# An accumulating DMA from GpSimd in place of a VectorE subtraction, in a spectral layer with a rational feed-forward block

## The chip, the cores and the metric

One core of one Trainium2 chip. The metric is device time in microseconds (us) of one execution of the kernel; the kernel before takes 1489.2 us, the median of three runs (1488.56 to 1489.77).

## The reference

The input is `x` of 4 x 3008 x 256. A real FFT runs along the sequence, each frequency's 256 channels go through a complex 256 x 256 mix with a soft threshold of 0.01, and the inverse FFT brings the sequence back. Then each of the 12032 tokens goes through a feed-forward block with a rational activation:

```
y = irfft(soft(rfft(x) @ (w_r + i w_i) + b))          # 4 x 3008 x 256
h = y @ w_in                                          # 12032 x 2048
P = a0 + a1*h + a2*h^2 + a3*h^3
Q = 1 + |b0|*|h| + |b1|*h^2 + 1e-6
out = (P / Q) @ w_out                                 # 12032 x 256
```

## The kernel before

**Blocks and units.** The tokens are cut into 26 blocks of 470 (the last has 282). A block goes through 8 units of 256 hidden channels each, so there are 208 units. A unit's tiles are 128 x 2 x 470, that is 128 x 940 (in the last block 128 x 564). The main loop (line 723) runs over the units in turn; in iteration i it issues the first product of unit i+1, the activation of units i, i-1 and i-2, and the second product of unit i-3. Everything is issued by hand in this order, and each engine works through its own list in order.

**One unit.** `g1_mm` (line 364): 12 matmuls of 470 columns give `h` in PSUM; two such tiles exist. ScalarE (`act_a`, `act_b`): m = |h| (line 394), w = |b1| m + |b0| (397), t = a3 h + a2 (398), then in the next iteration y = (v + C0)^2 (404) and its reciprocal square root (406), which is 1/Q. GpSimd: v = w m (399), so Q = v + C0. VectorE (`dve_a`): t = t h (411), t = (t + a1) h (413), so P = t + a0.

**Two ways to finish a unit** (`dve_b`). In mode "C" the quotient is split in two parts, both in a 32-bit format that TensorE multiplies in one pass: hi = (t + a0) y (423), p = (v + C0) hi (426), t = (t + a0) - p (428), lo = t y (431): six VectorE operations with the two of `dve_a`. The second product `g2_mm` (464) then has 12 matmuls: the high and low half of `w_out` with hi, the high half with lo. In mode "4" VectorE refines y twice (434, 436) and writes one full-precision tile g (440): five operations, and the second product has 4 matmuls of four passes each, shown in the profile as 8 records.

**Which unit takes which.** All units take "C" as long as FFT work of the later sequences is left. Once it is used up (`alone`), the table `TAIL = "4C444C44"` gives six of the eight units of a block mode "4". For these GpSimd joins halves of `w_out` again (line 801).

**FFT work beside the units.** The first sequence's FFT, mix and inverse stand before the loop. Those of the other three are cut into tasks (`fft_tasks`), which a planner spreads over the units by cost, so that TensorE's work per unit is level. Each block also needs its last inverse step (`i2_task`, lines 330 and 247), issued at units 5 and 6 of the block before. All DMAs are issued from SyncE.

**VectorE's order.** In iteration i: t h and (t + a1) h of unit i (any FFT step between them), line 428 of unit i-2, line 423 of unit i-1, line 431 of unit i-2, line 426 of unit i-1. GpSimd's v of unit i may overwrite its buffer only when line 426 (or 436) of unit i-2 has read it.

Of the kernel before, what the change touches and what calls it, by code (L numbers as in the profile page):

```python
# [25 lines left out]
FU = 2  # L26
UB = NFC // FU
LAM = 0.01
MODES = "CCCCCCCC"
TAIL = "4C444C44"  # L30
WARM = 38
FILL = 8
HC = (0, 0, 3, 3, 3, 3, 3, 3, 3, 3, 3, 3)
HM = (0, 0, 4, 4, 4, 4, 4, 4, 4, 4, 4, 4, 0, 0)
I2Q = (5, 6)
SPLIT = [q for q in range(UB) if MODES[q] != "4"]
WHOLE = [q for q in range(UB) if MODES[q] == "4"]
BACK = [q for q in SPLIT if TAIL[q] == "4"]
C0 = float(np.float32(1.0) + np.float32(1e-6))


# [59 lines left out]
def spectral_moe(ctx, tc, t, out):  # L101
# [17 lines left out]
    wout = const.tile([128, len(WHOLE), FU, D], F32, name="wout") if WHOLE else None  # L119
    win = {}  # L120
    wsp = {}
    back = f2.rearrange("p k f -> p (k f)").rearrange("p (k i f) -> p k i f", i=FU, f=D)
    ca, cna, cb = (small[:, k:m] for k, m in ((264, 268), (268, 272), (272, 274)))

    v32 = lambda ap: ap.bitcast(F32)
    early = [1]
# [218 lines left out]
    def width(u):  # L345
        return len(blocks[u // UB]) * TJ
# [20 lines left out]
    joined = []  # L367
    alone = []

    def mode(u):  # L370
        if u not in modes:
            q = u % UB
            four = TAIL[q] == "4" and (q in WHOLE or q in joined) and u != nb * UB - 1
            modes[u] = MODES[q] if not alone else "4" if four else "C"
        return modes[u]

    modes = {}
    rate = {}

    def load_rates():  # L380
        for k, src in (("b", cb[:1, 1:2]), ("a", ca[:1, 3:4]), ("na", cna[:1, 3:4])):
            rate[k] = nc.scalar.alloc_register(f"rate_{k}")
            nc.scalar.reg_load(rate[k], src.bitcast(I32))

    def fresh(nm, bufs):
        return mp.tile([128, FU, TB], F32, tag=nm, name=nm, bufs=bufs)

    def act_a(u):
        w = width(u)
# [24 lines left out]

    def dve_b(u):
        d = un[u]
        w = width(u)
        y, v, tt = (d[k] for k in ("y", "v", "t"))
        stt = nc.vector.scalar_tensor_tensor
        a0 = d["a"][:, 0:1]  # L420
        if mode(u) == "C":
            hi = fresh("g", 4)[:, :, :w].bitcast(F32R)
            stt(out=hi, in0=tt, scalar=a0, in1=y, op0=ALU.add, op1=ALU.mult)  # L423
            yield
            p = fresh("p", 1)[:, :, :w]
            stt(out=p, in0=v, scalar=C0, in1=v32(hi), op0=ALU.add, op1=ALU.mult)  # L426
            yield
            stt(out=tt, in0=tt, scalar=a0, in1=p, op0=ALU.add, op1=ALU.subtract)  # L428
            yield
            lo = fresh("g", 4)[:, :, :w].bitcast(F32R)  # L430
            nc.vector.tensor_tensor(out=lo, in0=tt, in1=y, op=ALU.mult)  # L431
            d["g"] = (hi, lo)
        else:
            stt(out=v, in0=v, scalar=C0, in1=y, op0=ALU.add, op1=ALU.mult)  # L434
            yield
            stt(out=y, in0=v, scalar=-2.0, in1=y, op0=ALU.add, op1=ALU.mult)  # L436
            yield
            yield
            g = fresh("g", 4)[:, :, :w]
            stt(out=g, in0=tt, scalar=a0, in1=y, op0=ALU.add, op1=ALU.mult)  # L440
            d["g"] = (g,)
# [4 lines left out]
    def g2_mm(u):  # L446
        n, q = divmod(u, UB)
        w = width(u)
        if n not in acc:
            acc[n] = [ps1.tile([128, 512], F32, tag=f"acc{e}", name=f"acc{e}") for e in range(2)]  # L450
            begun[n] = 0
        g = un.pop(u)["g"]
        ops = []
        for i in range(FU):
            if len(g) == 2:
                wh, wl = (wsp[q][:, i, z, :] for z in range(2))
                ops += [(wh, g[0][:, i]), (wh, g[1][:, i]), (wl, g[0][:, i])]
            else:
                w1 = wout[:, WHOLE.index(q), i, :] if q in WHOLE else back[:, BACK.index(q), i, :]
                ops.append((w1, g[0][:, i]))  # L460
# [39 lines left out]
    def from_f64(raw, kind, q):  # L500
# [11 lines left out]
        if kind == "whole":  # L512
            tt(out=wout[:, WHOLE.index(q)].rearrange("p k f -> p (k f)").bitcast(U32), in0=e, in1=r, op=ALU.add)
            yield
            return
# [9 lines left out]
    with tc.manual_schedule():  # L525
# [47 lines left out]
        jobs += [("whole", q, w_out[:, FU * q:FU * q + FU, :]) for q in WHOLE]  # L573
        jobs += [("wsp", q, w_out[:, FU * q:FU * q + FU, :]) for q in SPLIT]
        raws = []
        running = []

        def more_raw(n):
            for kind, q, src in jobs[len(raws):len(raws) + n]:
                if kind == "whole":  # L580
                    raw = raw_pool.tile([128, 2, 256], mybir.dt.int64, tag="raw", name="raw")
                else:
                    raw = const.tile([128, 2, 256], mybir.dt.int64, tag=f"{kind}{q}", name=f"raw_{kind}{q}")
# [59 lines left out]
        for p in range(np_ + 3):  # L643
# [79 lines left out]
        for i in range(-1, nu + 4):  # L723
# [59 lines left out]
            for g in live:  # L783
                drain(g)
            drain(da)
            next(prev, None)
            if i >= nu:
                drain(prev)
            next(db, None)
            drain(prev)  # L790
            next(db, None)
            held -= freed
            if len(cur) < 8 and 1 < nextb < B and (nextb, 0) not in xin:
                load_x(nextb, 0)
                load_x(nextb, 1)
            if i >= 0 and not cur and nextb == B:
                alone.append(1)
            left = [z for j, z in enumerate(BACK) if z not in joined and f2_done.get(B - 1, 0) >= 2 * j + 2]
            if left and not storing(i):
                j = BACK.index(left[0])  # L800
                nc.gpsimd.tensor_tensor(out=back[:, j], in0=v32(wsp[left[0]][:, :, 0]), in1=v32(wsp[left[0]][:, :, 1]), op=ALU.add)
                joined.append(left[0])
# [31 lines left out]
```

## Time and profile before

| | us |
|---|---|
| median of three runs | 1489.2 |
| the profiled execution | 1491.45 |
| its span in the profile | 1489.7 |
| TensorE busy | 1464.5 (98%) |
| VectorE busy | 1386.9 (93%) |
| ScalarE busy | 1214.5 (82%) |
| GpSimd busy | 478.4 (32%) |

In the span there are three stretches after a start of 120 us: the units with FFT work beside them (120.1 to 1119.1 us), the 56 units without it (to 1449.1 us), and the last block with what follows it. TensorE's granted clock is 1.00 of full speed in both long stretches. Busy times of VectorE and ScalarE hold a small overlap: an operation that does not depend on the one before starts some 0.08 us before that one's end.

### The profile page before, as it was taken

To read this page: it belongs to the slowest core of one execution; us is meant where nothing else is said; L and a number is where in the kernel's file an instruction comes from. 1 tells how busy PE (TensorE), PEld (TensorE's weight loads), DVE (VectorE), ACT (ScalarE), POOL (GpSimd) and SP (SyncE) were. 2 spreads that over 40 slices of the span, in tenths; PEclk is the share of its full clock that TensorE was granted. 3 is DMA by queue.
4 is the path that set the end of the run, shared out by engine and by line. 5 is a ranking of instruction groups with operands and counts; after the bars stand their busy time and mean duration, and the time that the engine had idled before them with its cause. 6 is when DMAs were issued, how large, how long until landed. Compare 5 with 4: busy or idle time off the path is not lost.

```text
span 1489.7 us, 19526 instructions
## 1 busy us (share of the span) xinstructions
PE 1464.5 (98%) x7323; PEld 1221.7 (82%) x7325; DVE 1386.9 (93%) x1347; ACT 1214.5 (82%) x1555; POOL 478.4 (32%) x230
## 2 busy tenths in 40 slices
PE   8999999999999999999999999999999999999998
PEld 4886999999888999999888998988987777777776
DVE  2667899999999999999999999999999999999998
ACT  2767888888888888888888888888888888888885
POOL 0102222332323233332323334333333333433332
PEclk9999999999999999999999999999999999999999
DMA  8934111111232111111232101011010000000000
GB/s 261 374 114 143 45 42 56 33 51 41 70 104 78 33 37 55 32 52 41 69 100 77 34 28 55 28 35 41 26 44 16 24 14 27 27 14 27 8 14 22
DMA packets 53458, 89.00 MB, mean 60 GB/s; under 512 B 4939, under 2 KB 37459, under 8 KB 53363
## 3 DMA queue, kind: packets, MB, share of 16 engines
q1 hardware_dynamic: 53363, 87.75, 19.0%
q8 instruction: 58, 0.95, 0.3%
q14 instruction: 37, 0.30, 0.1%
HBM read 50.25 MB, written 37.49 MB: 59 GB/s over the span
## 4 chain that ended last, share of the span: by engine, by line
PE 74%; DVE 11%; issue 7%; ACT 3%; DMA 0%; POOL 0%; SPq 0%; ACTq 0%; DVEq 0%; POOLq 0%
PE acc L464 30%; PE h L364 28%; PE pft L268 6%; PE pi L330 3%; DVE t L411 3%; DVE t L428 2%; DVE p L426 2%; PE pft L171 2%; PE pft L286 2%; PE pft L225 2%; DVE t L413 1%; PE pi L247 1%; DVE y L436 1%; DVE v L434 1%; PE pft L247 0%
## 5 line engine op out<-in xcount | busy, mean ns | idle before, releaser
L399 POOL TENSOR_TENSOR v<-w,m 128x940 f32<-128x940 f32 (+1 forms) x208 | 455.8, 2191 | 913.3 <-DVE p L426 514.5
L364 PE MATMUL h<-xsh,win 128*128 128x470 f32 (+1 forms) x1664 | 449.9, 392 | 2.5 <-DVE t L413 2.2
L464 PE MATMUL acc<-g,wsp 128*128 128x470 f32 (+1 forms) x1908 | 433.2, 375 | 3.4 <-DVE g L431 3.1
L464 PEld LDWEIGHTS acc<-g,wsp 128*128 128x128 f32 x1908 | 357.5, 189 | 53.5 <-DVE g L431 5.6
L364 PEld LDWEIGHTS h<-xsh,win 128*128 128x128 f32 x1664 | 304.2, 190 | 63.2 <-issue 23.6
L411 DVE TENSOR_TENSOR t<-t,h 128x940 f32<-128x940 f32 (+1 forms) x208 | 231.1, 1111 | 29.0 <-ACT t L398 28.8
L404 ACT ACTIVATE y<-v 128x940 f32<-128x940 f32 (+1 forms) x207 | 201.9, 975 | 66.8 <-POOL v L399 66.1
L413 DVE SCALAR_TENSOR_TENSOR t<-t,small,h 128x940 f32<-128x940 f32 (+1 forms) x208 | 244.8, 1177 | 6.1
L394 ACT ACTIVATE m<-h 128x940 f32<-128x940 f32 (+1 forms) x208 | 195.4, 939 | 60.5 <-PE h L364 55.4
L364 PE MATMUL h<-xsl,win 128*128 128x470 f32 (+1 forms) x832 | 242.0, 372 | 0.0
L397 ACT ACTIVATE w<-m,small 128x940 f32<-128x940 f32 (+1 forms) x208 | 220.1, 1058 | 0.0
L398 ACT ACTIVATE t<-h,small 128x940 f32<-128x940 f32 (+1 forms) x208 | 212.3, 1021 | 0.0
L406 ACT ACTIVATE y<-y 128x940 f32<-128x940 f32 (+1 forms) x207 | 202.5, 978 | 0.0
L423 DVE SCALAR_TENSOR_TENSOR g<-t,small,y 128x940 fp32r<-128x940 f32 (+1 forms) x158 | 192.6, 1219 | 0.0
L428 DVE SCALAR_TENSOR_TENSOR t<-t,small,p 128x940 f32<-128x940 f32 (+1 forms) x159 | 188.3, 1184 | 0.0
L431 DVE TENSOR_TENSOR g<-t,y 128x940 fp32r<-128x940 f32 (+1 forms) x158 | 178.0, 1127 | 10.9 <-PE acc L464 10.7
L426 DVE SCALAR_TENSOR_TENSOR p<-v,g 128x940 f32<-128x940 f32 (+1 forms) x159 | 178.5, 1122 | 0.2
L364 PEld LDWEIGHTS h<-xsl,win 128*128 128x128 f32 x832 | 155.2, 188 | 20.7 <-DVE xsl L341 0.2
L464 PE MATMUL acc<-g,f 128*128 128x470 f32 (+1 forms) x392 | 156.8, 542 | 1.5 <-DVE g L440 1.4
L464 PEld LDWEIGHTS acc<-g,f 128*128 128x128 f32 x392 | 73.5, 189 | 60.0 <-issue 52.7
L268 PE MATMUL pft<-wrh,x 128*128 128x256 f32 x288 | 76.5, 288 | 0.8 <-ACT pft L155 0.8
L268 PE MATMUL pft<-wih,x 128*128 128x256 f32 x288 | 75.0, 283 | 0.0
(94 smaller groups left out, 1450.1 us busy)
## 6 DMA issues: line engine op xcount, KB each, us to landing
xin<-in_x SPq DMA_DIRECT2D x32, 384.0 KB, 4.2
s<-zt SPq DMA_DIRECT2D x48, 256.0 KB, 2.2
out_t<-ob SPq DMA_DIRECT2D x50, 235.0 KB, 2.2
ct<-s SPq DMA_DIRECT2D x21, 480.0 KB, 4.6
s<-a SPq DMA_DIRECT2D x48, 192.0 KB, 2.8
bt<-s SPq DMA_DIRECT2D x36, 256.0 KB, 2.9
raw_win<-in_w_in SPq DMA_DIRECT2D x8, 512.0 KB, 10.6
raw_wsp<-in_w_out SPq DMA_DIRECT2D x8, 512.0 KB, 8.7
```

The costliest lines, as they stand in the source:

```text
L268: nc.tensor.matmul(out=pt[:, k, :], lhsT=l, rhs=r, start=False, stop=n == len(ops) - 1, skip_group_check=True)
L364: nc.tensor.matmul(out=h[:, i, :w], lhsT=l, rhs=r, start=k == 0, stop=k == len(halves) // FU - 1)
L397: nc.scalar.activation(out=d["w"], in_=d["m"], func=ACTF.Identity, scale=rate["b"], bias=cb[:, 0:1])
L398: nc.scalar.activation(out=d["t"], in_=h, func=ACTF.Identity, scale=rate["a" if mode(u) == "C" else "na"], bias=a[:, 2:3])
L399: nc.gpsimd.tensor_tensor(out=d["v"], in0=d["w"], in1=d["m"], op=ALU.mult)
L404: nc.scalar.activation(out=d["y"], in_=d["v"], func=ACTF.Square, bias=C0)
L406: nc.scalar.activation(out=d["y"], in_=d["y"], func=ACTF.Abs_reciprocal_sqrt)
L411: nc.vector.tensor_tensor(out=tt, in0=tt, in1=h, op=ALU.mult)
L413: nc.vector.scalar_tensor_tensor(out=tt, in0=tt, scalar=d["a"][:, 1:2], in1=h, op0=ALU.add, op1=ALU.mult)
L426: stt(out=p, in0=v, scalar=C0, in1=v32(hi), op0=ALU.add, op1=ALU.mult)
L428: stt(out=tt, in0=tt, scalar=a0, in1=p, op0=ALU.add, op1=ALU.subtract)
L464: nc.tensor.matmul(out=acc[n][e][:, :w], lhsT=l[:, e * 128:(e + 1) * 128], rhs=r, start=begun[n] == 1 and k == 0, stop=begun[n] == UB and ...
```

## The change

Line 428 goes. In its place `p` is written into `v` with the other sign, and GpSimd issues a DMA that adds the 128 x 940 tile `v` to `t` in SBUF. lo then takes (t + a0) y in one step. The signs are turned by loading w as -(|b1| m + |b0|) (`ncb`), so that v = -(Q - C0); y = (v - C0)^2 is unchanged. The tiles `w` and `p` go; `v` gets 4 buffers in place of 2, and the pieces `g` 5 in place of 4. Mode "4", its table and the join on GpSimd go: every unit is split. The very last unit adds on VectorE. In the loop both steps of unit i-1 (hi, p) now come before lo of unit i-2.

```diff
-        for nm, bufs in (("m", 2), ("w", 2), ("t", 4), ("v", 2)):
+        for nm, bufs in (("m", 2), ("v", 4), ("t", 4)):
...
-        nc.scalar.activation(out=d["w"], in_=d["m"], func=ACTF.Identity, scale=rate["b"], bias=cb[:, 0:1])
...
-        nc.gpsimd.tensor_tensor(out=d["v"], in0=d["w"], in1=d["m"], op=ALU.mult)
+        nc.scalar.activation(out=d["v"], in_=d["m"], func=ACTF.Identity, scale=rate["b"], bias=ncb[:, 0:1])
+        nc.scalar.activation(out=d["t"], in_=h, func=ACTF.Identity, scale=rate["a"], bias=ca[:, 2:3])
+        nc.gpsimd.tensor_tensor(out=d["v"], in0=d["v"], in1=d["m"], op=ALU.mult)
...
-        if mode(u) == "C":
...
+        piece = lambda: fresh("g", 5)[:, :, :width(u)].bitcast(F32R)
+        hi = piece()
+        stt(out=hi, in0=tt, scalar=ca[:, 0:1], in1=y, op0=ALU.add, op1=ALU.mult)
+        yield
+        stt(out=v, in0=v, scalar=-C0, in1=v32(hi), op0=ALU.add, op1=ALU.mult)
+        if u == nb * UB - 1:
+            nc.vector.tensor_tensor(out=tt, in0=tt, in1=v, op=ALU.add)
+        else:
+            nc.gpsimd.dma_start(out=tt, in_=v, accum_op=ALU.add)
+        yield
+        lo = piece()
+        stt(out=lo, in0=tt, scalar=ca[:, 0:1], in1=y, op0=ALU.add, op1=ALU.mult)
+        d["g"] = (hi, lo)
...
             drain(da)
-            next(prev, None)
-            if i >= nu:
-                drain(prev)
+            next(db, None)
             next(db, None)
             drain(prev)
-            next(db, None)
+            if i >= nu:
+                drain(db)
```

VectorE before, two neighbouring units of the stretch without FFT work (the numbers are buffers of the tiles; equal numbers are one tile):

```order
L411 TENSOR_TENSOR t_10074<-t_10074,h_10017 128x940
L413 SCALAR_TENSOR_TENSOR t_10074<-t_10074,small_69,h_10017 128x940
L434 SCALAR_TENSOR_TENSOR v_10033<-v_10033,y_10077 128x940
L440 SCALAR_TENSOR_TENSOR g_10090<-t_9989,small_69,y_10035 128x940
L436 SCALAR_TENSOR_TENSOR y_10077<-v_10033,y_10077 128x940
L411 TENSOR_TENSOR t_10111<-t_10111,h_10059 128x940
L413 SCALAR_TENSOR_TENSOR t_10111<-t_10111,small_69,h_10059 128x940
L423 SCALAR_TENSOR_TENSOR g_10126<-t_10074,small_69,y_10114 128x940
L440 SCALAR_TENSOR_TENSOR g_10128<-t_10032,small_69,y_10077 128x940
L426 SCALAR_TENSOR_TENSOR p_10130<-v_10075,g_10126 128x940
```

The same place now:

```order
L392 TENSOR_TENSOR t_10073<-t_10073,h_10012 128x940
L394 SCALAR_TENSOR_TENSOR t_10073<-t_10073,small_69,h_10012 128x940
L402 SCALAR_TENSOR_TENSOR g_10095<-t_10027,small_69,y_10075 128x940
L404 SCALAR_TENSOR_TENSOR v_10026<-v_10026,g_10095 128x940
L411 SCALAR_TENSOR_TENSOR g_10099<-t_9975,small_69,y_10029 128x940
L392 TENSOR_TENSOR t_10116<-t_10116,h_10058 128x940
L394 SCALAR_TENSOR_TENSOR t_10116<-t_10116,small_69,h_10058 128x940
L402 SCALAR_TENSOR_TENSOR g_10138<-t_10073,small_69,y_10118 128x940
L404 SCALAR_TENSOR_TENSOR v_10072<-v_10072,g_10138 128x940
L411 SCALAR_TENSOR_TENSOR g_10142<-t_10027,small_69,y_10075 128x940
```

Line 402 (hi) and line 404, which reads the hi just written, are now neighbours; before, an operation on another unit's tiles stood between lines 423 and 426. Line 411 (lo) reads the t to which the DMA of the iteration before has added.

GpSimd before, in the same stretch:

```order
L399 TENSOR_TENSOR v_10724<-w_10722,m_10721 128x940
L399 TENSOR_TENSOR v_10760<-w_10758,m_10757 128x940
L399 TENSOR_TENSOR v_10796<-w_10794,m_10793 128x940
L399 TENSOR_TENSOR v_10839<-w_10837,m_10836 128x940
L399 TENSOR_TENSOR v_10889<-w_10887,m_10886 128x940
```

and now:

```order
L380 TENSOR_TENSOR v_10297<-v_10297,m_10296 128x940
L408 DMA t_10247<-v_10246 128x940
L380 TENSOR_TENSOR v_10348<-v_10348,m_10347 128x940
L408 DMA t_10298<-v_10297 128x940
L380 TENSOR_TENSOR v_10400<-v_10400,m_10399 128x940
L408 DMA t_10349<-v_10348 128x940
```

Between two multiplications there is now the issue of a DMA, for the unit two before the one multiplied next (in iteration i: v of unit i, then the DMA of unit i-1, then v of unit i+1).

## Rows read from the trace of the kernel before

**Rows 1.** The page, its busy times: us, share, instructions.

```profile
PE 1464.5 (98%) x7323; PEld 1221.7 (82%) x7325; DVE 1386.9 (93%) x1347; ACT 1214.5 (82%) x1555; POOL 478.4 (32%) x230
```

**Rows 2.** By stretch: start:end, length, busy PE, PEld, DVE, ACT, POOL; clock, DMA share, GB/s.

```profile
120.10:1119.10 999.00, 992.52 (x5229) 876.05 (x5230) 965.79 (x894) 851.23 (x1083) 332.03 (x150) 1.00 0.17 52
1119.10:1449.10 330.00, 329.04 (x1324) 237.32 (x1323) 321.64 (x295) 277.23 (x323) 123.83 (x56) 1.00 0.06 19
```

**Rows 3.** VectorE's line 411 by stretch, once per unit: busy (count).

```profile
120.10:1119.10 999.00, 162.29 (x144) 1.00 0.17 52
1119.10:1449.10 330.00, 62.91 (x56) 1.00 0.06 19
```

**Rows 4.** Chain that ended last, 880 to 905 us, by line.

```profile
by line: PE acc L464 41.3%; PE h L364 32.6%; PE pft L268 12.4%; PE pi L330 4.5%; PE pft L225 3.6%; PE pft L286 3.5%; PE pi L247 1.7%; PE pft L247 0.9%
```

**Rows 5.** Waits of TensorE for VectorE, 120 to 1119 us: total, times, longest.

```profile
PE h L364 <- DVE t L413: 1.4, 2, 0.8
...
PE acc L464 <- DVE g L431: 0.2, 1, 0.2
```

**Rows 6.** Chain around one block without FFT work: start us, us, what.

```profile
1208.59 3.16 PE acc L464 x8
...
1214.31 2.56 PE acc L464 x12
1216.87 2.59 PE h L364 x12
...
1239.18 1.13 PE pi L330 x10
...
1242.88 0.21 PE pi L247
```

**Rows 7.** VectorE in order of time in that block: start us, us, what.

```profile
1218.12 1.12 DVE L436 SCALAR_TENSOR_TENSOR y<-v,y 128x940 f32<-128x940 f32 x1
1219.17 1.12 DVE L411 TENSOR_TENSOR t<-t,h 128x940 f32<-128x940 f32 x1
1220.32 1.19 DVE L413 SCALAR_TENSOR_TENSOR t<-t,small,h 128x940 f32<-128x940 f32 x1
...
1222.50 1.19 DVE L440 SCALAR_TENSOR_TENSOR g<-t,small,y 128x940 f32<-128x940 f32 x1
1223.61 1.13 DVE L436 SCALAR_TENSOR_TENSOR y<-v,y 128x940 f32<-128x940 f32 x1
```

**Rows 8.** VectorE at the start of the loop, lines 423 and 426 as neighbours.

```profile
126.94 1.19 DVE L423 SCALAR_TENSOR_TENSOR g<-t,small,y 128x940 fp32r<-128x940 f32 x1
128.24 1.14 DVE L426 SCALAR_TENSOR_TENSOR p<-v,g 128x940 f32<-128x940 f32 x1
```

**Rows 9.** GpSimd in order of time, same block.

```profile
1219.39 2.19 POOL L399 TENSOR_TENSOR v<-w,m 128x940 f32<-128x940 f32 x1 [3.30 <-DVE y L436]
```

**Rows 10.** ScalarE in order of time, same block.

```profile
1221.62 0.99 ACT L404 ACTIVATE y<-v 128x940 f32<-128x940 f32 x1 [0.88 <-POOL v L399]
...
1223.48 1.02 ACT L398 ACTIVATE t<-h,small 128x940 f32<-128x940 f32 x1
```

**Rows 11.** SyncE's issue of one DMA, in order of time.

```profile
568.53 0.46 SPq L314 DMA_DIRECT2D ct<-s  x1
```

**Rows 12.** DMA issues: count, KB each, median us from issue to landing.

```profile
out_t<-ob SPq DMA_DIRECT2D x50, 235.0 KB, 2.2
ct<-s SPq DMA_DIRECT2D x21, 480.0 KB, 4.6
```

**Rows 13.** VectorE in the last block, in order of time.

```profile
1469.21 0.74 DVE L411 TENSOR_TENSOR t<-t,h 128x564 f32<-128x564 f32 x1
...
1472.74 0.73 DVE L411 TENSOR_TENSOR t<-t,h 128x564 f32<-128x564 f32 x1
...
1481.47 0.80 DVE L423 SCALAR_TENSOR_TENSOR g<-t,small,m 128x564 fp32r<-128x564 f32 x1
1482.38 0.75 DVE L426 SCALAR_TENSOR_TENSOR p<-v,g 128x564 f32<-128x564 f32 x1
```

More of the change, by code (lines that the diff above doesn't have):

```diff
@@ L28 @@
 LAM = 0.01
-MODES = "CCCCCCCC"
-TAIL = "4C444C44"
 WARM = 38
@@ L35 @@
 I2Q = (5, 6)
-SPLIT = [q for q in range(UB) if MODES[q] != "4"]
-WHOLE = [q for q in range(UB) if MODES[q] == "4"]
-BACK = [q for q in SPLIT if TAIL[q] == "4"]
 C0 = float(np.float32(1.0) + np.float32(1e-6))
@@ L118, in spectral_moe @@
     wmix = {n: const.tile([128, 2, D], F32R, name=n) for n in ("wrh", "wrl", "wih", "wil")}
-    wout = const.tile([128, len(WHOLE), FU, D], F32, name="wout") if WHOLE else None
     win = {}
     wsp = {}
-    back = f2.rearrange("p k f -> p (k f)").rearrange("p (k i f) -> p k i f", i=FU, f=D)
-    ca, cna, cb = (small[:, k:m] for k, m in ((264, 268), (268, 272), (272, 274)))
+    ca, ncb, cb = (small[:, k:m] for k, m in ((264, 268), (268, 270), (272, 274)))
     v32 = lambda ap: ap.bitcast(F32)
@@ L365, in g1_mm @@
         un[u] = {"h": h}
[L367 to L377, printed above, removed]
     rate = {}
     def load_rates():
-        for k, src in (("b", cb[:1, 1:2]), ("a", ca[:1, 3:4]), ("na", cna[:1, 3:4])):
+        for k, src in (("b", ncb[:1, 1:2]), ("a", ca[:1, 3:4])):
             rate[k] = nc.scalar.alloc_register(f"rate_{k}")
@@ L395, in act_a @@
         yield
-        d["a"] = a = ca if mode(u) == "C" else cna
-        nc.scalar.activation(out=d["w"], in_=d["m"], func=ACTF.Identity, scale=rate["b"], bias=cb[:, 0:1])
-        nc.scalar.activation(out=d["t"], in_=h, func=ACTF.Identity, scale=rate["a" if mode(u) == "C" else "na"], bias=a[:, 2:3])
-        nc.gpsimd.tensor_tensor(out=d["v"], in0=d["w"], in1=d["m"], op=ALU.mult)
+        nc.scalar.activation(out=d["v"], in_=d["m"], func=ACTF.Identity, scale=rate["b"], bias=ncb[:, 0:1])
+        nc.scalar.activation(out=d["t"], in_=h, func=ACTF.Identity, scale=rate["a"], bias=ca[:, 2:3])
+        nc.gpsimd.tensor_tensor(out=d["v"], in0=d["v"], in1=d["m"], op=ALU.mult)
     def act_b(u):
@@ L403, in act_b @@
         d["y"] = fresh("m", 2)[:, :, :width(u)] if u == nb * UB - 1 else fresh("y", 3)[:, :, :width(u)]
-        nc.scalar.activation(out=d["y"], in_=d["v"], func=ACTF.Square, bias=C0)
+        nc.scalar.activation(out=d["y"], in_=d["v"], func=ACTF.Square, bias=-C0)
         yield
@@ L412, in dve_a @@
         yield
-        nc.vector.scalar_tensor_tensor(out=tt, in0=tt, scalar=d["a"][:, 1:2], in1=h, op0=ALU.add, op1=ALU.mult)
+        nc.vector.scalar_tensor_tensor(out=tt, in0=tt, scalar=ca[:, 1:2], in1=h, op0=ALU.add, op1=ALU.mult)
     def dve_b(u):
         d = un[u]
-        w = width(u)
         y, v, tt = (d[k] for k in ("y", "v", "t"))
         stt = nc.vector.scalar_tensor_tensor
-        a0 = d["a"][:, 0:1]
-        if mode(u) == "C":
[L422 to L432, printed above, removed]
-        else:
[L434 to L441, printed above, removed]
+        piece = lambda: fresh("g", 5)[:, :, :width(u)].bitcast(F32R)
[5 more added lines that the diff above has]
+            nc.vector.tensor_tensor(out=tt, in0=tt, in1=v, op=ALU.add)
+        else:
+            nc.gpsimd.dma_start(out=tt, in_=v, accum_op=ALU.add)
[3 more added lines that the diff above has]
+        d["g"] = (hi, lo)
     acc = {}
@@ L454, in g2_mm @@
         for i in range(FU):
[L455 to L460, printed above, removed]
+            wh, wl = (wsp[q][:, i, z, :] for z in range(2))
+            ops += [(wh, g[0][:, i]), (wh, g[1][:, i]), (wl, g[0][:, i])]
         begun[n] += 1
@@ L493, in spectral_moe @@
     pro3 = pro_stack.enter_context(tc.tile_pool(name="pro3", bufs=3))
-    raw_pool = pro_stack.enter_context(tc.tile_pool(name="raw", bufs=len(WHOLE))) if WHOLE else None
     pro2 = pro_stack.enter_context(tc.tile_pool(name="pro2", bufs=2))
@@ L511, in from_f64 @@
         yield
[L512 to L515, printed above, removed]
         tt(out=e, in0=e, in1=r, op=ALU.add)
@@ L572, in spectral_moe @@
         jobs = [("win", q, w_in[:, :, 256 * q:256 * q + 256]) for q in range(UB)]
-        jobs += [("whole", q, w_out[:, FU * q:FU * q + FU, :]) for q in WHOLE]
-        jobs += [("wsp", q, w_out[:, FU * q:FU * q + FU, :]) for q in SPLIT]
+        jobs += [("wsp", q, w_out[:, FU * q:FU * q + FU, :]) for q in range(UB)]
         raws = []
@@ L579, in more_raw @@
             for kind, q, src in jobs[len(raws):len(raws) + n]:
[L580 to L583, printed above, removed]
+                raw = const.tile([128, 2, 256], mybir.dt.int64, tag=f"{kind}{q}", name=f"raw_{kind}{q}")
                 nc.sync.dma_start(out=raw, in_=src)
@@ L687, in spectral_moe @@
             if p == 8:
-                nc.vector.tensor_scalar(out=cna, in0=ca, scalar1=-1.0, scalar2=None, op0=ALU.mult)
                 nc.scalar.activation(out=cb, in_=cb, func=ACTF.Abs)
+                nc.vector.tensor_scalar(out=ncb, in0=cb, scalar1=-1.0, scalar2=None, op0=ALU.mult)
         load_rates()
@@ L716, in load @@
         def load(i):
-            z = 0.5 * storing(i) + 2.36 + (0.0 if i < 3 else 3.16 if MODES[(i - 3) % UB] == "4" else 2.36)
+            z = 0.5 * storing(i) + 2.36 + (0.0 if i < 3 else 2.36)
             return z + (1.24 if i % UB in I2Q else 0.0)
@@ L795, in spectral_moe @@
                 load_x(nextb, 1)
[L796 to L802, printed above, removed]
             if 0 <= i < nu and q == 1 and n + 1 < nb:
```

## The prediction

> **What bounds the kernel now.** I read the page's busy times first, then the busy times by stretch, then the chain of waits inside each long stretch, and only then single instructions in order of time. The page shows two engines near full: TensorE at 98% and VectorE at 93% [rows 1]. An average does not say which of them sets the pace, so the next view is by stretch.
>
> In the stretch with FFT work TensorE is busy 992.5 of 999.0 us, VectorE 965.8 [rows 2]. The chain there, followed back, holds TensorE lines alone [rows 4], and TensorE waited for VectorE for 1.4 + 0.2 = 1.6 us in all of it [rows 5]. The reader is to see that VectorE, though almost full, delays nobody there: a faster VectorE can give back those 1.6 us and little more.
>
> The stretch without FFT work has 56 units in 330.0 us [rows 2, 3], 5.89 us each. The chain around one block shows TensorE without a gap: six second products of mode "4" at 3.16 us, two of mode "C" at 2.56, eight first products at about 2.57, two inverse steps of 1.13 + 0.21 [rows 6]: 18.96 + 5.12 + 20.56 + 2.68 = 47.3 us for 8 units, 5.92 each, which is the measured pace. Here too TensorE sets it, but with work that the change takes away.
>
> **The change part by part.**
>
> *TensorE.* In the FFT stretch its list is the same. Without FFT work six of eight second products go from 3.16 to 2.56 us: 8 x 2.56 + 20.56 + 2.68 = 43.7 us per block, 5.47 per unit. If nothing else bound, that would be worth 56 x (5.89 - 5.47) = 24 us.
>
> *VectorE.* A unit now takes five operations everywhere. I take the distance from start to start, since ends overlap the next start. Line 411 to 413, which reads what 411 has just written, is 1.15 us; an operation with the coefficient column to its independent neighbour is 1.11 (440 to 436); one with a constant is 1.05 (436 to 411) [rows 7]. The new neighbours hi and p depend on each other. Lines 423 and 426 stood so once at the loop's start, 1.30 us apart [rows 8], 0.19 more than hi costs now. So a unit takes 1.15 + 1.11 + 1.30 + 1.05 + 1.11 = 5.72 us. In the FFT stretch VectorE's 965.8 us over 144 units are 6.71 per unit; less 1.11 for the subtraction, plus 0.19, plus 0.06 because lo now carries the coefficient column, that is 5.85, against a pace of 999.0 / 144 = 6.94. Cover is ample there, and TensorE stays the wall: gain 1.6 us. Without FFT work 5.72 is above TensorE's 5.47, so VectorE becomes the bound: 56 x 5.72 = 320.3 in place of 330.0, gain 9.7 us.
>
> *The DMA, its latency.* lo of a unit stands one whole iteration behind the p that starts its DMA: between them lie lo of the unit before, two steps of `dve_a`, hi and p, 5.72 us of VectorE. A latency L up to that costs nothing. Beyond it VectorE waits W in each iteration, with L = 5.72 + 2W, because the wait lengthens the iteration it hides in; so a unit costs (L - 5.72) / 2 more. Queued behind the waiting lo are `dve_a` of the next unit (which frees `h` for the first product after) and hi. In the FFT stretch L may reach 5.85 + 2 x (6.94 - 5.85) = 8.0 before TensorE feels it. No accumulating DMA is in this trace. Nearest rows: 235 KB from SBUF land after 2.2 us, 480 KB into SBUF after 4.6 [rows 12]; this one moves 481 KB and reads its destination too. Ends: 2.2 + 0.46 = 2.7 us, and twice 4.6 plus an issue of 2.2, 11.4. I take the row with the same size, 4.6, plus the issue below: L = 5.6, just inside. The Trainium skill ("DMA: Bandwidth & Descriptors", section on the anatomy of one DMA) gives for a DMA from GpSimd about 2.0 us plus the bytes at 436 GB/s, by which 481 KB would take an estimated 3.1 us and the sum would be the same.
>
> *The DMA, its issue on GpSimd.* While GpSimd issues (d), v of the next unit waits behind it. The loop: the last reader of v, line 436, ends at 1219.24 [rows 7], GpSimd starts at 1219.39 and takes 2.19 [rows 9], ScalarE's square starts at 1221.62, its t ends at 1224.50 [rows 10]: 5.26 us. In the new order line 404 releases the DMA, so d comes in; then `dve_a`, hi and p follow, 1.15 + 1.11 + 1.30 + 1.13 = 4.69, and about 0.1 for the start. The whole, 10.05 + d, has two units to run in: a pace of 5.72 allows d up to 1.4 us. In the FFT stretch two units are 13.9 us and d may be near 3. Bounds for d: SyncE's issue, 0.46 [rows 11], and a whole GpSimd multiplication, 2.19 [rows 9]; I take 1.0, the geometric middle. Below nothing it cannot be, since it stands in GpSimd's list.
>
> *The rest.* Of the buffers, v of unit i also waits for the DMA of unit i-4, more than two units earlier, which costs nothing at the L taken. lo comes after hi and p now; the second product that reads it stands two iterations behind, as before. In the last block a unit takes 3.53 us on VectorE, five operations of about 0.71; the pair hi, p is 0.91 apart there [rows 13], so 8 x 0.2 = 1.6 us more, and at the end lo of the last unit but one waits for its DMA with little before it: 0.9, together +2.5. The copies, constants and joins that go (GpSimd's, off the path) count nothing.
>
> *Sum.* -1.6 - 9.7 + 2.5 = -8.8 us. The profiled execution took 1491.45 us (span 1489.7), 2.25 above the median; 1482.65 less 2.25 is 1480.4: I predict 1480 us.
>
> **The rivals.**
>
> *A. GpSimd becomes the bound (slower).* For it: GpSimd is in the loop with 0.4 us to spare at d = 1.0, and ScalarE already waits 0.88 us for v in this block [rows 10]. Against: GpSimd idles 3.30 us before each multiplication [rows 9]. At d = 2.2, the upper bound, a unit takes (10.05 + 2.2) / 2 = 6.12: 56 x 0.23 = 13 us lost without FFT work, with -1.6 and +2.5 about 1503 us. It decides for slower from d = 1.7 (5.88 a unit). GpSimd's multiplication runs its 2.19 us beside lines 411 and 413, which keep their 1.15 us and 1.19 us [rows 7, 9], so the trace shows no stop of a whole operation. The Trainium skill ("SBUF — State Buffer", section "Who interferes with whom") says that a VectorE operation with two SBUF inputs and a GpSimd one that reads SBUF block each other for the whole operation; if issuing were held so, d would be an estimated 1.0 + 1.2, which is this rival.
>
> *B. The transfer is late (slower).* If the second read costs a third of the transfer more, L is 1.0 + 1.3 x 4.6 = 7.0 and a unit takes 6.36: 56 x 0.47 = 26, about 1516 us. It turns the change from L = 6.0. The DMA engines are far from full (share 0.06 without FFT work [rows 2]), which speaks against queueing; the unknown rate of adding speaks for it. At L = 11.4 a unit would take 8.6 in both stretches, (8.6 - 6.94) x 144 + (8.6 - 5.89) x 56 = 390 us more; nothing points there.
>
> *C. TensorE keeps the pace.* If hi and p stand closer than 1.30 (p's wait was seen once), VectorE falls to TensorE's 5.47: 24 us in place of 9.7, about 1466 us.
>
> *D. A draw.* L or d lies just past its limit, a unit takes 5.85 to 5.95, and the gain is eaten: about 1489 us.
>
> **How the numbers follow.** Forecast 0.43 (its own range 1474 to 1486), A 0.15, B 0.17, C 0.13, D 0.12. A measurement tells no change from about 0.2%, 3 us. Faster: forecast and C, 0.56; same: D, 0.12; slower: A and B, 0.32. The range goes from C, 1466, to short of B, 1512; what lies outside is most of B and a tail of C.
>
> **What would show it.** After: TensorE's busy share in the FFT stretch unchanged and that stretch within 3 us of 999.0; units without FFT work 5.7 us apart with VectorE full and TensorE waiting about 0.25 us per unit; lines 402 and 404 1.30 apart; no wait of line 411 for the DMA; GpSimd's issue near 1 us. Wrong would be: waits of line 411 for DMA in most units (B), waits of ScalarE's square for GpSimd that grow by more than 0.4 us per unit (A), units at 5.5 (C), or an FFT stretch that moves by over 5 us either way.

## The result and the profile after

The changed kernel takes 1507.25 us (median of four runs, 1501.95 to 1511.85), against 1489.33 for the kernel before beside it: a ratio of 1.012, interval 1.0085 to 1.0155. It became slower by about 18 us; the forecast was 1480. The profiled execution took 1508.81 us, its span is 1507.0.

The busy times of the page after, beside [rows 1], and four of its groups (line, engine, operation, count | busy us, mean ns | idle before, releaser):

```profile
PE 1450.8 (96%) x7521; PEld 1259.8 (84%) x7521; DVE 1272.3 (84%) x1189; ACT 1214.2 (81%) x1555; POOL 656.5 (44%) x431
...
L380 POOL TENSOR_TENSOR v<-v,m 128x940 f32<-128x940 f32 (+1 forms) x208 | 501.3, 2410 | 73.5 <-ACT v L378 50.4
L408 POOL DMA_DIRECT2D t<-v x207 | 184.6, 892 | 684.7 <-DVE v L404 684.7
...
L411 DVE SCALAR_TENSOR_TENSOR g<-t,small,y 128x940 fp32r<-128x940 f32 (+1 forms) x207 | 264.5, 1278 | 17.0 <-DMA t<-v 15.6
L402 DVE SCALAR_TENSOR_TENSOR g<-t,small,y 128x940 fp32r<-128x940 f32 (+1 forms) x207 | 253.0, 1222 | 1.6 <-ACT y L387 1.6
...
t<-v POOLq DMA_DIRECT2D x200, 470.0 KB, 4.4
...
out_t<-ob SPq DMA_DIRECT2D x50, 235.0 KB, 3.9
ct<-s SPq DMA_DIRECT2D x21, 480.0 KB, 6.3
```

VectorE lost 115 us of work; besides TensorE's weight loads (PEld) only GpSimd has more to do than before. The two numbers that the prediction did not have came out near its choice: the issue takes 0.89 us (1.0 was taken), the transfer lands 4.4 us after it (4.8 after line 404's end; 5.6 was taken, 5.72 was the limit). The transfers beside it became slower, `out_t` from 2.2 to 3.9 us and `ct` from 4.6 to 6.3 [rows 12]; none of the waits below is for those. What stands out is the mean of line 411: 1278 ns, where the other operations of its kind take 1.19 us.

The same three stretches, cut where VectorE starts units 0, 144 and 200 (columns as in [rows 2]):

```profile
116.40:1120.20 1003.80, 994.17 (x5224) 879.62 (x5225) 842.11 (x753) 850.37 (x1082) 447.57 (x288) 0.99 0.55 120
1120.20:1457.20 337.00, 316.75 (x1493) 269.28 (x1491) 324.86 (x282) 277.00 (x322) 176.39 (x114) 0.98 0.49 99
1457.20:1507.00 49.80, 34.09 (x205) 30.57 (x203) 41.15 (x47) 24.57 (x40) 21.09 (x17) 0.92 0.43 76
```

Before they were 999.0, 330.0 and 40.6 us. So the stretch with FFT work lost 4.8 us, the 56 units without it 7.0, the last block 9.2; the start gave 3.7 back. Together that is the 17.3 us between the spans.

**One unit in some twenty.** VectorE after, in order of time (start us, us, what, [idle before, releaser]):

```profile
1298.64 1.13 DVE L392 TENSOR_TENSOR t<-t,h 128x940 f32<-128x940 f32 x1
1299.81 1.19 DVE L394 SCALAR_TENSOR_TENSOR t<-t,small,h 128x940 f32<-128x940 f32 x1
1300.92 1.26 DVE L402 SCALAR_TENSOR_TENSOR g<-t,small,y 128x940 fp32r<-128x940 f32 x1
1302.29 1.14 DVE L404 SCALAR_TENSOR_TENSOR v<-v,g 128x940 f32<-128x940 f32 x1
1304.04 3.92 DVE L411 SCALAR_TENSOR_TENSOR g<-t,small,y 128x940 fp32r<-128x940 f32 x1 [0.61 <-DMA t<-v]
1307.88 1.12 DVE L392 TENSOR_TENSOR t<-t,h 128x940 f32<-128x940 f32 x1
```

and GpSimd in the same place:

```profile
1298.64 2.53 POOL L380 TENSOR_TENSOR v<-v,m 128x940 f32<-128x940 f32 x1
1303.84 0.89 POOL L408 DMA_DIRECT2D t<-v  x1 [2.67 <-DVE v L404]
1304.45 2.50 POOL L380 TENSOR_TENSOR v<-v,m 128x940 f32<-128x940 f32 x1
```

lo (line 411) waited 0.61 us for its transfer, and then took 3.92 us in place of 1.19. It ends at 1307.96; GpSimd's multiplication (line 380) ends at 1306.95, 1.01 us earlier. Read hi (line 402) against the multiplication before it: that ends at 1301.17, hi at 1302.18, 1.01 us later again, and hi took 1.26 us. Both look as if VectorE's work on them began only when GpSimd was done (1.01 us is close to the 1.19 that such an operation takes alone). The unit cost 9.24 us from one line 392 to the next; its neighbours take 5.81. Nine of the 207 lo's are this long (2.3 to 3.95 us), and all nine end 1.0 us after a multiplication's end.

TensorE pays a second time. Its rows there:

```profile
1300.00 2.73 PE L431 MATMUL acc<-g,wsp 128*128 128x470 f32 x12
...
1308.01 4.17 PE L431 MATMUL acc<-g,wsp 128*128 128x470 f32 x11 [2.49 <-DVE g L411]
```

It stood still 2.49 us for lo, and the 11 products after it took 0.38 us each in place of 0.23. The granted clock over those products is 0.57 of full speed, so they ran mostly at the lower level, 1.2 GHz in place of 2.4 (columns as in [rows 2]); before had 1.00 in both long stretches.

```profile
1308.00:1312.00 4.00, 3.99 (x11) 3.46 (x12) 3.85 (x4) 3.76 (x4) 0.00 (x0) 0.57 0.00 0
```

### The profile page after: what moved, and what is told of

It is laid out like the page before. It is cut to its first block, busy times and chain, and to the rows that moved or that the text cites. A ratio compares the mean times of both kernels' runs of the same rounds, so it can differ in the third digit from the quotient of the medians.

```text
span 1507.0 us, 20592 instructions
## 1 busy us (share of the span) xinstructions
PE 1450.8 (96%) x7521; PEld 1259.8 (84%) x7521; DVE 1272.3 (84%) x1189; ACT 1214.2 (81%) x1555; POOL 656.5 (44%) x431
## 4 chain that ended last, share of the span: by engine, by line
PE 58%; issue 16%; POOL 15%; DVE 3%; ACT 3%; DMA 2%; POOLq 0%; ACTq 0%; DVEq 0%
PE acc L431 21%; PE h L357 21%; POOL v L380 11%; PE pft L261 7%; POOL t L408 4%; PE pi L323 3%; PE pft L279 2%; PE pft L218 2%; DMA t<-v 2%; PE pft L164 1%; DVE g L411 1%; PE pft L240 0%; PE pi L240 0%; ACT m L376 0%; DVE e L478 0%
## 5 line engine op out<-in xcount | busy, mean ns | idle before, releaser
L431 PE MATMUL acc<-g,wsp 128*128 128x470 f32 (+1 forms) x2496 | 580.1, 380 | 41.1 <-DVE g L411 36.6
L431 PEld LDWEIGHTS acc<-g,wsp 128*128 128x128 f32 x2496 | 470.0, 192 | 118.7 <-DVE g L411 51.2
L380 POOL TENSOR_TENSOR v<-v,m 128x940 f32<-128x940 f32 (+1 forms) x208 | 501.3, 2410 | 73.5 <-ACT v L378 50.4
L408 POOL DMA_DIRECT2D t<-v x207 | 184.6, 892 | 684.7 <-DVE v L404 684.7
L357 PE MATMUL h<-xsh,win 128*128 128x470 f32 (+1 forms) x1664 | 436.4, 384 | 0.3 <-ACT xsh L326 0.3
L411 DVE SCALAR_TENSOR_TENSOR g<-t,small,y 128x940 fp32r<-128x940 f32 (+1 forms) x207 | 264.5, 1278 | 17.0 <-DMA t<-v 15.6
L402 DVE SCALAR_TENSOR_TENSOR g<-t,small,y 128x940 fp32r<-128x940 f32 (+1 forms) x207 | 253.0, 1222 | 1.6 <-ACT y L387 1.6
L404 DVE SCALAR_TENSOR_TENSOR v<-v,g 128x940 f32<-128x940 f32 (+1 forms) x208 | 233.7, 1124 | 23.8 <-DVE g L402 0.9
L378 ACT ACTIVATE v<-m,small 128x940 f32<-128x940 f32 (+1 forms) x208 | 220.1, 1058 | 0.0
L323 PEld LDWEIGHTS pi<-small,ct 96*128 96x128 f32 x512 | 65.0, 191 | 3.2 <-ACT a L148 0.7
L323 PE MATMUL pi<-small,ct 96*128 96x94 f32 (+1 forms) x512 | 66.0, 276 | 0.0
```

Of the source, the lines that this page charges most:

```text
L378: nc.scalar.activation(out=d["v"], in_=d["m"], func=ACTF.Identity, scale=rate["b"], bias=ncb[:, 0:1])
L380: nc.gpsimd.tensor_tensor(out=d["v"], in0=d["v"], in1=d["m"], op=ALU.mult)
L402: stt(out=hi, in0=tt, scalar=ca[:, 0:1], in1=y, op0=ALU.add, op1=ALU.mult)
L404: stt(out=v, in0=v, scalar=-C0, in1=v32(hi), op0=ALU.add, op1=ALU.mult)
L408: nc.gpsimd.dma_start(out=tt, in_=v, accum_op=ALU.add)
L411: stt(out=lo, in0=tt, scalar=ca[:, 0:1], in1=y, op0=ALU.add, op1=ALU.mult)
```

## Theories and experiments

*The lock (theory; "exclusion" in the expectations).* A VectorE operation with two inputs in SBUF and GpSimd's multiplication exclude each other. Lines 392 and 394 read h in PSUM, lines 402, 404 and 411 read SBUF alone. A lo that is late meets the multiplication that the DMA's issue has just let go, and is held to its end. *Latency (rival).* The transfer alone is late, and a unit pays what it is late. *Issue (rival).* GpSimd's issue of the DMA stops VectorE, or makes v late, and that holds the rest.

Stretches of all kernels, from their profiles (us; VectorE's starts of units 0, 144, 200). The last column is the distance at which most of the 56 units follow each other; for before, whose two modes alternate, it is the mean:

| kernel | start | FFT | 56 units | last block | normal unit |
|---|---|---|---|---|---|
| before | 120.1 | 999.0 | 330.0 | 40.6 | 5.89 |
| after | 116.4 | 1003.8 | 337.0 | 49.8 | 5.81 |
| e1_no_mult | 117.4 | 992.8 | 322.7 | 48.2 | 5.66 |
| e2_guard | 117.5 | 992.7 | 335.0 | 52.0 | 5.97 |
| e3_no_wait | 116.2 | 991.7 | 324.5 | 43.8 | 5.79 |
| e4_before_shift | 116.5 | 1117.7 | 387.7 | 49.7 | 6.68 |
| e5_square | 118.6 | 992.9 | 324.9 | 48.0 | 5.73 |
| e6_square_before | 116.0 | 1001.4 | 329.7 | 40.7 | |
| e7_split_all_dve | 118.2 | 996.8 | 368.8 | 46.5 | 6.58 |
| e8_late | 119.1 | 994.1 | 324.6 | 48.7 | 5.70 |

**e1_no_mult.** After, without GpSimd's multiplication: v stays w, so y and p hold other values; the DMAs stay.

```diff
-        nc.gpsimd.tensor_tensor(out=d["v"], in0=d["v"], in1=d["m"], op=ALU.mult)
```

> GpSimd's multiplication is left out (v is the ScalarE result w itself); everything else, the accumulating DMA too, stays. Three theories of the 18 us lost. Exclusion: GpSimd's multiplication and a VectorE operation whose two inputs lie in SBUF run one after the other, whichever begins first; a lo that waited a little for its DMA finds the multiplication begun and stands until its end, and hi is held a little in every unit. Then no lo is over 1.3 us, hi to p is 1.30 in place of 1.37, a unit without FFT work takes 5.73 us in place of 5.81, one of the last block 3.8 in place of 4.5, and the time is about 1482 us. Latency (rival B of the prediction): the DMA's landing alone costs the time; it lands as late as now, so the time stays within 5 us of 1507. Issue: the DMA's issue on GpSimd stops VectorE; lo still reaches 2 us and more where it starts during an issue, and the time stays above 1500.

Measured: 1483.23 us (1481.38 to 1483.28), ratio 0.9957 (0.994 to 0.9974). VectorE's lines 401 (hi) and 410 (lo) there (that kernel's numbers are one lower):

```profile
L401 DVE SCALAR_TENSOR_TENSOR g<-t,small,y 128x940 fp32r<-128x940 f32 (+1 forms) x207 | 243.9, 1178 | 0.8 <-ACT y L386 0.8
L410 DVE SCALAR_TENSOR_TENSOR g<-t,small,y 128x940 fp32r<-128x940 f32 (+1 forms) x207 | 243.9, 1178 | 19.8 <-DMA t<-v 19.2 <-PE h L357 0.5
```

lo still waits for its transfer, 19.2 us in all against 15.6 in after, but its mean is back at 1178 ns and no lo takes over 1.20 us. The lateness is there, and its amplification is gone: 24 us. The DMA's issues all stay, so an issue alone does not make lo long. The small parts of the lock's forecast were off: hi to p is 1.23 us in place of 1.30, and a unit of the last block takes some 4.2 in place of 3.8. The run takes all of GpSimd's arithmetic out, so v is earlier as well; the next runs separate that.

**e2_guard.** After, with a one-column GpSimd operation that reads lo ahead of each multiplication, so that a late lo always comes first.

```diff
         d["g"] = (hi, lo)
+        if u < nb * UB - 2:
+            nc.gpsimd.tensor_scalar(out=tiny[:, u % 2, :1], in0=v32(lo)[:, 0, :1], scalar1=1.0, scalar2=0.0, op0=ALU.mult, op1=ALU.add)
```

> One tiny GpSimd operation (128 x 1, reading lo of the unit two before) is put ahead of each multiplication, so that the multiplication cannot begin before lo is done; nothing is left out. Exclusion: a late lo now costs its lateness alone (under 0.8 us) in place of 3 us, no lo is over 1.3 us, the stretch without FFT work falls from 337 to about 327 us, and the time to about 1493 us. Latency: the landings are as late as before and the guard only adds to GpSimd's list: 1507 us or more. Issue: lo still reaches 2 us where it meets an issue; 1503 us or more.

Measured: 1498.7 us (1497.33 to 1500.07), ratio 1.0064 (1.0047 to 1.0081). GpSimd, then VectorE, in one normal unit:

```profile
1300.92 0.89 POOL L409 DMA_DIRECT2D t<-v  x1 [2.67 <-DVE v L405]
1301.79 0.26 POOL L415 TENSOR_SCALAR tiny<-g 128x1 f32<-128x1 f32 x1
1301.94 2.28 POOL L381 TENSOR_TENSOR v<-v,m 128x940 f32<-128x940 f32 x1
```

```profile
1303.81 1.43 DVE L403 SCALAR_TENSOR_TENSOR g<-t,small,y 128x940 fp32r<-128x940 f32 x1
1305.34 1.14 DVE L405 SCALAR_TENSOR_TENSOR v<-v,g 128x940 f32<-128x940 f32 x1
```

No lo is over 1.2 us, though v comes later than in after: the issue theory falls here too. The FFT stretch is as good as in e1 (992.7). But the 56 units take 335.0 us, where the lock's forecast was 327 (and 1493 in all): the multiplication now starts 0.4 us later in every unit (1.02 us after the issue's start, 0.61 in after) and holds hi each time: it ends at 1304.22, hi at 1305.24, 1.02 later. Without FFT work a unit takes 5.97 us.

**e3_no_wait.** After, with the DMA moving 128 x 8 to a scratch tile; the subtraction is left out. The multiplication stays, the lateness of lo goes.

```diff
-            nc.gpsimd.dma_start(out=tt, in_=v, accum_op=ALU.add)
+            nc.gpsimd.dma_start(out=tiny[:, u % 2], in_=v[:, 0, :8], accum_op=ALU.add)
```

> The accumulating DMA moves 128 x 8 values into a scratch tile that nobody reads; lo waits for no DMA (the subtraction of p is left out). GpSimd's list and issue stay. Exclusion and latency: no lo is late, none is over 1.3 us. Exclusion beside that: hi still meets the end of the multiplication (1.26 us), a unit without FFT work stays at 5.8, and one of the last block stays above 4 us; about 1492 us. Latency: 5.72 per unit and 3.8 in the last block, about 1481 us. Issue: long lo's remain, since the issue is the same; above 1500 us.

Measured: 1478.35 us (1478.03 to 1483.58), ratio 0.994 (0.9921 to 0.9959); no long lo. The time is below both forecasts, 1492 by the lock and 1481 by latency, and nearer to latency's. The units decide between the two: 5.79 us, where the lock said 5.8 and latency 5.72, and 4.2 in the last block, where the lock said above 4 and latency 3.8. So the long lo's need both: without the multiplication (e1) or without lateness (e3) there are none. The hold of hi, which needs no lateness, stays: a unit takes 5.79.

**e4_before_shift.** The kernel before, with a DMA of 128 x 8 to a scratch tile issued on GpSimd ahead of each multiplication (after line 426, and likewise after line 436). All of before's work is done; only the multiplication moves.

```diff
             stt(out=p, in0=v, scalar=C0, in1=v32(hi), op0=ALU.add, op1=ALU.mult)
+            nc.gpsimd.dma_start(out=tiny[:, u % 2], in_=p[:, 0, :8], accum_op=ALU.add)
```

> The kernel before, with one added accumulating DMA of 128 x 8 values into a scratch tile, issued by GpSimd after line 426 (or 436) of each unit, so that its multiplication begins 0.9 us later; nobody waits for the DMA. Exclusion: the multiplication, which lay beside lines 411 and 413 (one input in PSUM), now reaches 0.9 us into line 428 or 434 (both inputs in SBUF) and holds it: VectorE goes from 6.7 to about 7.6 us a unit with FFT work and to about 6.6 without; about 1620 us. Latency and issue: the loop over GpSimd grows by 0.9 us in two units, 5.9 per unit at most, and the time stays within 15 us of 1489.

Measured: 1673.41 us in one run, 184 us above before. GpSimd, then VectorE, in order of time (line 424 is before's 423, line 430 its 428):

```profile
1304.07 2.51 POOL L400 TENSOR_TENSOR v<-w,m 128x940 f32<-128x940 f32 x1
...
1310.75 2.49 POOL L400 TENSOR_TENSOR v<-w,m 128x940 f32<-128x940 f32 x1
```

```profile
1305.24 2.35 DVE L424 SCALAR_TENSOR_TENSOR g<-t,small,y 128x940 fp32r<-128x940 f32 x1
...
1311.93 2.32 DVE L430 SCALAR_TENSOR_TENSOR t<-t,small,p 128x940 f32<-128x940 f32 x1
```

No transfer is waited for here, and the two operations that the multiplication overlaps took 2.3 us in place of 1.19. They end at 1307.59 and 1314.25, 1.01 us after the multiplications' ends at 1306.58 and 1313.24. Latency and issue allowed some 1504 us at most. The lock's own forecast, about 1620, was 53 us short: on average a unit takes 7.76 us in the FFT stretch and 6.92 without, in place of 7.6 and 6.6, and the last block 9.1 more than before. So the lock was in the kernel before as well, and the multiplication just missed it. The row that shows how narrowly, of before (line 434 has two SBUF inputs; the multiplication of [rows 9] ends at 1221.58):

```profile
1221.43 1.14 DVE L434 SCALAR_TENSOR_TENSOR v<-v,y 128x940 f32<-128x940 f32 x1
```

It ends at 1222.57, 0.99 us after the multiplication: there the hold was just zero.

**e5_square.** After, with v made by ScalarE alone: |b1| m^2 + |b0| m is a square less a constant, (s m + c)^2 - c^2 with s = sqrt(|b1|) and c = |b0| / (2 s). One ScalarE operation takes the place of line 378, and the multiplication goes; nothing is left out, the constants change.

```diff
-        nc.scalar.activation(out=d["v"], in_=d["m"], func=ACTF.Identity, scale=rate["b"], bias=ncb[:, 0:1])
+        nc.scalar.activation(out=d["v"], in_=d["m"], func=ACTF.Square, scale=rate["b"], bias=qc[:, 2:3])
...
-        nc.gpsimd.tensor_tensor(out=d["v"], in0=d["v"], in1=d["m"], op=ALU.mult)
```

> The changed kernel with GpSimd's multiplication replaced, nothing left out: ScalarE makes v as the square of (sqrt|b1| m + c) with c = |b0| / (2 sqrt|b1|) in place of the step that made w, and the constants of the two steps that read v are changed to match, as columns read from SBUF. GpSimd then only issues DMAs. Exclusion: as in the run without the multiplication; no lo over 1.3 us, hi to p 1.30, the stretches 993, 323 and 48 us, 1483 us within 4 (p reads a column now, 0.06 us a unit, at most 3 us more). Latency alone: 1500 us or more, since every landing stays.

Measured: 1485.02 us (1483.03 to 1486.22), ratio 0.9966 (0.9952 to 0.998). Its wait of lo (us in all, times, longest) and the groups of lo and hi:

```profile
DVE g L411 <- DMA t<-v: 16.4, 22, 1.8
```

```profile
L411 DVE SCALAR_TENSOR_TENSOR g<-t,small,y 128x940 fp32r<-128x940 f32 (+1 forms) x207 | 244.3, 1180 | 17.3 <-DMA t<-v 16.4 <-PE acc L431 0.8
L402 DVE SCALAR_TENSOR_TENSOR g<-t,small,y 128x940 fp32r<-128x940 f32 (+1 forms) x207 | 244.2, 1180 | 0.5 <-ACT y L387 0.5
```

The same lateness as after (15.6 us, 19 times, at most 2.3) and no long operation: lo's 264.5 us became 244.3, hi's 253.0 became 244.2. By latency alone this run would have been as slow as after.

**e6_square_before.** The same edit in the kernel before (w goes, and v gets 4 buffers).

> The kernel before with the same replacement of GpSimd's multiplication by a square on ScalarE; no accumulating DMA, both modes stay, nothing left out. If TensorE bound the kernel before, as read, ScalarE's waits for GpSimd go (67 us, all beside TensorE) and the time stays within 6 us of 1489, faster rather than slower. If VectorE's or GpSimd's loop bound it after all, the gain is above 10 us.

Measured: 1490.69 us, ratio 1.0009 (1.000 to 1.0018). Where the multiplication held no operation, taking it away wins nothing. What e5 wins over after is not the removal of work as such.

**e7_split_all_dve.** The kernel before with every unit split and the subtraction still on VectorE: one half of the change alone.

```diff
-TAIL = "4C444C44"
+TAIL = "CCCCCCCC"
```

> The other part of the change alone: the kernel before with every unit split (its table set to C throughout) and the subtraction left on VectorE; no DMA. VectorE bounds the stretch without FFT work at six operations, 6.58 us a unit in place of 5.89: 368 in place of 330 us; the FFT stretch stays at 999; about 1530 us in all by each theory. It is the price that the DMA's five operations have to earn back.

Measured: 1532.09 us in one run. Splitting alone costs 43 us, 38.8 of them in the 56 units (six VectorE operations, 6.58 us a unit), 5.9 in the last block. The rest of the change, the DMA with its order and buffers, takes one operation out and gives back 25 of them; with the lock out of the way (e5) it gives back 47.

**e8_late.** e5, with lo and the second product one iteration later, hi and lo in tiles of their own, so that a transfer has longer to land (main lines of the edit).

```diff
             next(db, None)
+            drain(older)
             next(db, None)
-            drain(prev)
```

> The kernel with the square on ScalarE, and lo one iteration later: VectorE's order is the two steps of dve_a, hi of unit i-1, lo of unit i-3, p of unit i-1, and the second product is issued for unit i-4. hi and p no longer stand side by side, and a DMA has more than a unit longer to land; m is made in v's tile to pay for a fourth y and a sixth piece; nothing is left out. If the 0.19 us between hi and p and the landings are what still holds the stretch without FFT work, a unit goes from 5.73 to 5.58 us there (TensorE needs 5.47): 323 to about 313 us, the FFT stretch stays at 993, the last block falls by 3 to 5 us, and the time is about 1471 us. If VectorE does not bound there, the stretch stays at 323 and the time at 1485.

Measured: 1484.9 us (1483.47 to 1488.27), ratio 0.9971 (0.9959 to 0.9983): no gain over e5, against the 1471 us and 5.58 a unit that were expected. Its waits:

```profile
ACT t L380 <- DVE gl L410: 52.9, 62, 1.6
```

VectorE's wait for the transfer fell to 3.6 us, but ScalarE's t now waits for lo of four units before, whose buffer it takes (t has 4). The wait changed its place. That it is what keeps a unit at 5.70 us is argued, not shown: more buffers of t were not tried.

Of the versions that leave nothing out, e5 and e8 beat both kernels, by some 4 us against before. Their square needs |b1| away from zero, since c divides by its root.

## Why the prediction was wrong

**The step that failed** is in rival A: "GpSimd's multiplication runs its 2.19 us beside lines 411 and 413, which keep their 1.15 us and 1.19 us [rows 7, 9], so the trace shows no stop of a whole operation." The rows are right and the conclusion is not: the sum put nothing in for GpSimd's multiplication holding hi and lo. Lines 411 and 413 read h from PSUM; no VectorE operation with two SBUF inputs stood beside a multiplication in those rows, so they could not show the stop.

The whole trace of before does show it, in five places that the prediction did not look at. Where GpSimd joins halves of w_out (line 801) right behind a multiplication, line 423 takes 2.23 to 2.25 us in place of 1.19. The first of the five, GpSimd, then VectorE:

```profile
854.83 2.20 POOL L801 TENSOR_TENSOR f<-wsp 128x512 f32<-128x512 f32 x1
```

```profile
855.79 2.25 DVE L423 SCALAR_TENSOR_TENSOR g<-t,small,y 128x940 fp32r<-128x940 f32 x1
```

The join ends at 857.03 and line 423 at 858.04, again 1.0 us later. e6, which has the joins and no multiplication, has six such operations.

The Trainium skill ("SBUF — State Buffer", section "Who interferes with whom") says just this: a VectorE operation with two SBUF inputs contends with a GpSimd one that reads SBUF, one with at most one SBUF input does not, outside the modes that use both of VectorE's ports. The trace agrees with both halves: lines 402, 411, 424 and 430 are held to 1.0 us past the multiplication's end, lines 392 and 394 (411 and 413 before) never. The prediction quoted the first half and used it only for the length of the DMA's issue, d.

The lock can hold either engine. On who waits, the Trainium skill says in the same section that the order of issue decides who is blocked. Of the 19 late lo's nine are long. Three others, with recorded starts 0.43 to 0.64 us ahead of the multiplication's, kept 1.20 us, and there the multiplication took 2.65 to 2.86 us in place of 2.5. One of the three, VectorE, then GpSimd:

```profile
1353.82 1.20 DVE L411 SCALAR_TENSOR_TENSOR g<-t,small,y 128x940 fp32r<-128x940 f32 x1 [0.59 <-DMA t<-v]
```

```profile
1354.25 2.86 POOL L380 TENSOR_TENSOR v<-v,m 128x940 f32<-128x940 f32 x1
```

For the remaining seven the multiplication came over 1.0 us later, or none was left. But the recorded starts alone do not decide: the lo at 1304.04 was 0.41 us ahead of its multiplication and one at 131.99 even 0.50, and both were held. Which moment of an operation counts, no run here shows.

**What the lock does to the sum.** It closes a loop through GpSimd in each unit: line 404 takes 1.14, GpSimd's issue starts 0.41 later, the multiplication 0.61 after that and runs 2.53, hi ends 1.01 after it, line 404 starts 0.11 later: 1.14 + 0.41 + 0.61 + 2.53 + 1.01 + 0.11 = 5.81 us, the measured pace. So rival A named the right engine, by another way and at another size: GpSimd became the bound with the issue at 0.89 us, not at 1.7. Rival A's 1503 us lies near the measured time by luck: it put its whole loss into the 56 units, and two thirds of the measured one stand in the other two stretches. By the same sum e2 gives 1.14 + 0.41 + 1.02 + 2.28 + 1.02 + 0.10 = 5.97, as measured. The forecast's loop, 10.05 + d over two units, was slacker, because in it hi waited for ScalarE's y alone, and the multiplication held nothing.

**The 56 units (-9.7 forecast, +7.0 measured).** 56 x 5.81 = 325.4 us, 4.6 under before. Three long lo's at 9.24 - 5.81 = 3.4 us put 10.3 on it, and 1.3 us are smaller waits. Undisturbed, the forecast was not far off: e1 has 322.7 and e5 324.9 against 320.3. In e1 two errors partly cancel: a unit is 5.66 us, shorter than the 5.72 forecast, and waits add some 6 us. The distance of hi and p, forecast as 1.30, is 1.23 there, 1.37 in after.

**The FFT stretch (-1.6 forecast, +4.8 measured).** The forecast took VectorE's slack, 1.1 us a unit, for cover. Five long lo's stand in this stretch, and two of them go far beyond that cover: TensorE stood still behind them for 4.10 and 3.36 us, and there its clock fell to the lower level. Against e1 the stretch is 11 us longer. TensorE's rows, and the stretches around them (columns as in [rows 2], granted clock 0.93 and 0.83):

```profile
136.00 4.68 PE L431 MATMUL acc<-g,wsp 128*128 128x470 f32 x11 [4.10 <-DVE g L411]
...
806.92 4.68 PE L431 MATMUL acc<-g,wsp 128*128 128x470 f32 x11 [3.36 <-DVE g L411]
```

```profile
100.00:150.00 50.00, 43.16 (x174) 30.67 (x173) 37.72 (x39) 36.26 (x48) 17.04 (x10) 0.93 0.64 167
...
800.00:820.00 20.00, 16.43 (x71) 13.97 (x69) 16.66 (x13) 13.50 (x19) 7.21 (x6) 0.83 0.53 115
```

Undisturbed (e1, e2, e3, e5) the stretch gains 6.1 to 7.3 us, more than forecast. The cuts are VectorE's starts, so some of that may be VectorE running closer behind TensorE; that is argued, not shown. e6 loses 2.4 us there and e7 gains 2.2, both without the DMA, so a difference of some 2 us says little.

**The last block (+2.5 forecast, +9.2 measured).** A unit takes 4.5 us, not 3.53 + 0.2, by the same loop through GpSimd, and one of the nine long lo's stands here, in a unit of 7.20 us. GpSimd, then VectorE, in one unit of after:

```profile
1486.64 1.21 POOL L408 DMA_DIRECT2D t<-v  x1 [1.89 <-DVE v L404]
1487.42 1.87 POOL L380 TENSOR_TENSOR v<-v,m 128x564 f32<-128x564 f32 x1
```

```profile
1488.35 1.55 DVE L402 SCALAR_TENSOR_TENSOR g<-t,small,y 128x564 fp32r<-128x564 f32 x1
1490.01 0.75 DVE L404 SCALAR_TENSOR_TENSOR v<-v,g 128x564 f32<-128x564 f32 x1
```

hi takes 1.55 us in place of 0.80, and the issue 1.21, more than for the larger tile. Taking the lock away alone helps little there (e1 48.2, e5 48.0), because then the transfer is late in most of the short units; making the transfer small leaves 43.8 (e3), where the issue is back at 0.89 us as well and hi is still held (1.2 us). Two limits lie close together, and the prediction had neither.

**What held.** TensorE's list and VectorE's count; d, and L by its median. But L went in as one value, so the forecast had no late transfer at all; of rival B's sign, lo waiting in most units, 19 waits in 207 units are there, up to 2.3 us. Lateness by itself is cheap, as forecast: e5 carries 16.4 us of such waits and is still faster than before. With the lock away e1 (1483.23) lies 3 us from the 1480 forecast, though by errors of both signs, an FFT stretch better than forecast and a last block worse.

## What to carry to other kernels

A trace in which two engines seem not to disturb each other may only show which operations stand side by side: look for the few long operations of a line, not only at its mean. Before anything is moved on GpSimd's list, look which VectorE operations with two SBUF inputs its work would then overlap, and count each as held to its end. A transfer given just enough time is late now and then, and what matters is what a late operation runs into; here 0.6 us became 3.4. Look for a closed loop through both engines as soon as a DMA's issue stands between two steps of GpSimd.

## What the runs showed of the hardware

- A held VectorE operation of 128 x 940 ends 1.01 us after GpSimd's multiplication, in after (hi and lo), e2 and e4 alike; one of 128 x 564 ends 0.61 us after it (after's last block).
- The accumulating DMA, SBUF to SBUF, of 470 KB lands 4.4 us after its issue from GpSimd (median); the issue takes 0.89 us, but 1.21 for 128 x 564, whose rows are two pieces of 282 in the tile.
- The multiplication itself is recorded at 2.5 us where the DMA's issue is just ahead of it (after, e4), 2.2 to 2.3 otherwise [rows 9] and in e2. Its record begins before the issue's ends (1304.45 and 1304.73), so that the two overlap by 0.28 us; whether this is all of the difference was not tested.
